# x turned by VectorE in 32x32 blocks that the store puts in place, with g moved into the division of x^T and a longer first phase

## The chip, the cores and the metric

One core of one Trainium2 chip. The metric is the time of one launch on the device in microseconds (us); the profile's span, without the launch's own ends, is about 1.8 us shorter. A ratio of two kernels is the mean time of one's fast runs over that of the other's fast runs of the same rounds, so it is not quite the ratio of the medians that stand beside it.

## The reference

```python
# q, k, v: (8, 8, 576, 64) float32; w_in (512, 2048), w_out (2048, 512): float64
kv  = einsum('bhsd,bhse->bhde', k, v)
o   = einsum('bhsd,bhde->bhse', q, kv)
o   = o / sqrt(mean(o * o, -1) + 1e-6) * g_norm             # g_norm: (64,)
x   = o.transpose(0, 2, 1, 3).reshape(4608, 512)
h   = x @ w_in
out = (maximum(h, 0) + log1p(exp(-abs(h)))) @ w_out         # softplus
```

## The kernel before

The 4608 rows are 36 tiles of 128, and 12 blocks of three tiles. The 2048 columns of the MLP are 16 chunks of 128. A *step* is one chunk of one block: 12 matmuls of 128x384 (L558; three factors of x^T and w_in for precision), softplus on ScalarE, a division of the result into three factors, and nine matmuls of 128x512 (L565). There are 192 steps, in three phases of 4, 6 and 6 chunks for all blocks; partial sums wait in DRAM between phases. Attention for all tiles is done in the first phase beside the steps, and x^T goes to DRAM, from which each later use loads it.

```python
PHASES = [range(0, 4), range(4, 10), range(10, 16)]
...
def split(ph, t, x, ready, pos):            # the division of x^T into three factors
    def high(): nc.scalar.activation(cols(0, F32R), x.tile, func=AF.Copy, scale=DOWN)                            # L410
    def low():  nc.vector.tensor_tensor(out=cols(1, F32R), in0=x.tile, in1=cols(0), op=ALU.subtract)             # L413
    def less(): nc.vector.scalar_tensor_tensor(out=cols(2, F32R), in0=cols(1), scalar=-RADIX, in1=cols(0), ...)  # L416
...
def rows(t):                                # attention of one tile
    def turn_q():                           # L490: four transposes on TensorE
    def out_rows():                         # L496: q^T by kv
    def norm():  nc.vector.tensor_tensor(out=x.tile, in0=o.tile, in1=r.tile..., op=ALU.mult)                     # L507
    def turn_x():
        y = new(xp, [P, KD, P])
        for p in range(KD):
            nc.tensor.transpose(y[:, p], pairs(x.tile, p), ident)                                                # L512
    ...
    a = add("PE", 440, turn_x, [a], pos + 0.5, [xp], [x])
    a = add("ACT", 700, lambda: nc.scalar.activation(new(xg, [P, KD, P]), xp.tile, func=AF.Identity, scale=g_col), ...)  # L526
    x_there[t] = add("SP", 350, lambda: nc.sync.dma_start(out=xd[t], in_=xg.tile.rearrange("p a t -> p (a t)")), ...)
    if t < AT_ONCE:                         # the first six tiles are divided at once, without DRAM
        split(0, t, xg, a, pos + 0.5)
def x_again(ph, t):                         # load x^T from DRAM and divide it
    ld = add("SP", 350, lambda: nc.sync.dma_start(out=new(xt, ...), in_=xd[t]), ...)
    split(ph, t, xt, ld, pos)
```

Every operation is recorded with a *position* (in steps). A small list scheduler in the kernel then orders each engine's instructions by buffers and positions at build time. The list `P0` holds the fitted positions: when each weight is fetched and converted, how early x is made. Tiles that TensorE writes lie in PSUM (the pool `ps` in the kernel), the others in SBUF (`sb`). Filler matmuls (L668) occupy TensorE where it has nothing else to do before the first step.

## Time and profile before

| | before |
|---|---|
| median of the first session, us | 938.43 |
| TensorE busy in the span of 936.5 us | 925.1 |
| TensorE idle from the first step (45.6 us) to the end of the first phase | 0.2 |
| DMA engines busy | 47% |
| first phase ends | 336 us |

### The profile page before, as it was taken

What the parts mean: (1) busy time and instruction counts of PE and PEld (TensorE: products, weight loads), DVE (VectorE), ACT (ScalarE), POOL (GpSimd) and SP (SyncE); (2) the same over time, 40 slices, a digit from 0 to 9 for tenths busy, and PEclk for the clock granted to TensorE, in tenths of its full rate; (3) what the DMA queues carried; (4) which work ended last, traced back from release to release, by engine and by line L of the source; (5) the groups of instructions that cost most, each with busy time, mean ns of one, the idle gap of its engine ahead of it and who ended that gap; (6) DMA issues with size and microseconds to landing.
All of it is one profiled execution on the core that took longest, in us unless ns stands there. A gap on an engine that the chain in (4) does not pass through costs nothing.

```text
span 936.5 us, 13571 instructions
## 1 busy us (share of the span) xinstructions
PE 925.1 (99%) x5019; PEld 837.3 (89%) x5019; DVE 601.5 (64%) x1045; ACT 449.3 (48%) x871; POOL 66.9 (7%) x42
## 2 busy tenths in 40 slices
PE   7999999999999999999999999999999999999998
PEld 5799999999999899989999999899999999999997
DVE  7888876777777667776767645485455554545443
ACT  5877766666666555544444332374323233232331
POOL 0331122212222000000000000000000000000000
PEclk9999999999999999999999999999999999999999
DMA  9999776786564444444343322343323333222221
GB/s 247 242 258 278 201 215 202 216 229 186 169 189 137 135 147 124 147 135 148 125 138 130 129 81 85 135 147 101 102 101 101 102 101 102 101 84 95 77 82 68
DMA packets 148673, 135.63 MB, mean 145 GB/s; under 512 B 86400, under 2 KB 102784, under 8 KB 148608
## 3 DMA queue, kind: packets, MB, share of 16 engines
q1 hardware_dynamic: 148448, 134.78, 47.0%
q8 instruction: 39, 0.64, 0.3%
q14 instruction: 26, 0.21, 0.1%
q10 hardware_dynamic: 160, 0.00, 0.0%
HBM read 93.85 MB, written 40.89 MB: 144 GB/s over the span
## 4 chain that ended last, share of the span: by engine, by line
PE 95%; DMA 2%; DVE 1%; ACT 1%; issue 0%; SPq 0%; ACTq 0%
PE h L558 43%; PE s L565 42%; PE o L472 3%; PE o L496 3%; PE tp L512 2%; PE tp L490 1%; DMA kvt<-in_v_dram 1%; DMA raw<-in_moe_w_out_dram 1%; DMA part<-xg 0%; PE s L496 0%; PE h L668 0%; DVE xv L413 0%; PE h L357 0%; DVE xv L416 0%; SPq L456 0%
## 5 line engine op out<-in xcount | busy, mean ns | idle before, releaser
L565 PE MATMUL s<-w,gv 128*128 128x512 f32 x1728 | 438.8, 396 | 0.0
L558 PE MATMUL h<-xv,w 128*128 128x384 f32 x2304 | 435.8, 337 | 0.0
L558 PEld LDWEIGHTS h<-xv,w 128*128 128x128 f32 x2304 | 405.6, 188 | 14.1
L565 PEld LDWEIGHTS s<-w,gv 128*128 128x128 f32 x1728 | 318.1, 188 | 57.1 <-issue 0.3
L578 ACT ACTIVATE g<-h 128x384 f32<-128x384 f32 x192 | 94.5, 492 | 393.4 <-PE h L558 380.7
L569 DVE TENSOR_TENSOR gv<-g,gv 128x384 fp32r<-128x384 f32 x192 | 107.0, 557 | 203.2 <-ACT gv L580 202.5
L573 DVE SCALAR_TENSOR_TENSOR gv<-gv 128x384 fp32r<-128x384 f32 x192 | 107.1, 558 | 6.2
L580 ACT ACTIVATE gv<-g 128x384 fp32r<-128x384 f32 x192 | 101.0, 526 | 6.7 <-PE s L565 1.2
L504 POOL TENSOR_TENSOR r<-r,half 128x8 f32<-128x8 f32 x36 | 66.2, 1840 | 228.8 <-DVE r L501 223.3
L413 DVE TENSOR_TENSOR xv<-xt,xv 128x512 fp32r<-128x512 f32 x102 | 70.1, 687 | 17.8 <-ACT xv L410 17.5
L416 DVE SCALAR_TENSOR_TENSOR xv<-xv 128x512 fp32r<-128x512 f32 x108 | 74.6, 691 | 3.2
L410 ACT ACTIVATE xv<-xt 128x512 fp32r<-128x512 f32 x102 | 62.6, 623 | 16.0 <-DMA xt<-x 16.0
L605 DVE SCALAR_TENSOR_TENSOR qT<-s,kvt 128x512 f32<-128x512 f32 x36 | 24.7, 687 | 28.2 <-PE s L565 26.0
L472 PE MATMUL o<-kvt,kvt 128*128 128x128 f32 x256 | 35.0, 281 | 3.7 <-DMA kvt<-in_v_dram 3.7
L472 PEld LDWEIGHTS o<-kvt,kvt 128*128 128x128 f32 x256 | 33.4, 195 | 5.8 <-issue 3.2
L496 PE MATMUL o<-kv_diag,qT 128*128 128x128 f32 (+1 forms) x296 | 36.9, 276 | 0.3 <-DVE kv_diag L480 0.3
L496 PEld LDWEIGHTS o<-kv_diag,qT 128*128 128x128 f32 (+1 forms) x296 | 34.4, 179 | 1.4 <-issue 0.6
L500 DVE TENSOR_REDUCE r<-x 128x8 f32<-128x512 f32 x36 | 24.6, 684 | 9.0 <-ACT x L520 8.7
L526 ACT ACTIVATE xg<-tp,g_col 128x512 f32<-128x512 f32 x36 | 24.7, 687 | 10.1 <-PE tp L512 9.8
L507 DVE TENSOR_TENSOR x<-o,r 128x512 f32<-128x512 f32 x33 | 22.7, 689 | 8.5 <-POOL r L504 8.2
L605 DVE SCALAR_TENSOR_TENSOR qT<-s,scale,kvt 128x512 f32<-128x512 f32 x12 | 9.0, 752 | 29.4 <-PE s L565 29.4
L515 ACT COPY qT<-tp 128x512 f32<-128x512 f32 x36 | 21.1, 586 | 11.2 <-PE tp L490 10.9
(68 smaller groups left out, 508.4 us busy)
## 6 DMA issues: line engine op xcount, KB each, us to landing
xt<-x SPq DMA_DIRECT2D x102, 256.0 KB, 2.9
kvt<-part SPq DMA_DIRECT2D x72, 256.0 KB, 4.2
x<-xg SPq DMA_DIRECT2D x36, 256.0 KB, 3.2
part<-xg SPq DMA_DIRECT2D x36, 256.0 KB, 3.3
part<-qT SPq DMA_DIRECT2D x36, 256.0 KB, 2.0
raw<-in_moe_w_in_dram SPq DMA_DIRECT2D x16, 512.0 KB, 5.3
kvt<-in_k_dram SPq DMA_DIRECT2D x64, 128.0 KB, 4.1
kvt<-in_v_dram SPq DMA_DIRECT2D x32, 256.0 KB, 4.1
```

The lines of the kernel that those rows point to most:

```text
L410: nc.scalar.activation(cols(0, F32R), x.tile, func=AF.Copy, scale=DOWN)
L413: nc.vector.tensor_tensor(out=cols(1, F32R), in0=x.tile, in1=cols(0), op=ALU.subtract)
L416: nc.vector.scalar_tensor_tensor(out=cols(2, F32R), in0=cols(1), scalar=-RADIX, in1=cols(0), op0=ALU.mult, op1=ALU.add)
L472: nc.tensor.matmul(kv[:, i if tail else p], lhsT=l, rhs=r, start=(p == 0 and i == 0), stop=tail, skip_group_check=True)
L496: nc.tensor.matmul(pairs(y[r0:r0 + n], p), lhsT=qT.tile[:, p, r0:r0 + n], rhs=kv_diag[b % 2][:, p], start=(p == 0), stop=True, skip_group_ ...
L504: nc.gpsimd.tensor_tensor(out=r.tile, in0=r.tile, in1=half, op=ALU.pow)
L558: nc.tensor.matmul(hp, lhsT=w_in.tile[:, i, kd * P:(kd + 1) * P], rhs=xv.tile[:, i, kd], start=(m == 0), stop=(m == 3 * KD - 1))
L565: nc.tensor.matmul(mine[i].tile, lhsT=gv.tile[:, m, i * P:(i + 1) * P], rhs=w_out.tile[:, m], start=(c == cs[0] and m == 0), stop=(c == cs ...
L569: nc.vector.tensor_tensor(out=gv.tile[:, 1], in0=g.tile, in1=gv.tile.bitcast(F32)[:, 0], op=ALU.subtract)
L573: nc.vector.scalar_tensor_tensor(out=gv.tile[:, 2], in0=f32[:, 1], scalar=-RADIX, in1=f32[:, 0], op0=ALU.mult, op1=ALU.add)
L578: a = add("ACT", 490, lambda: nc.scalar.activation(new(g, [P, NT]), h.tile, func=AF.Softplus, scale=1.0 + E), [a], s, [g], [h])
L580: a = add("ACT", 530, lambda: nc.scalar.activation(new(gv, [P, 3, NT], F32R)[:, 0], g.tile, func=AF.Copy, scale=DOWN), [a], s, [gv])
```

## The change

Intent: take x's transposes off TensorE, the bound, and spread attention, which loads VectorE and the DMA engines, over more steps.

```diff
-    PHASES = [range(0, 4), range(4, 10), range(10, 16)]
+    LATE = 4
+    ENDS = [[0] * n_blocks, [4] * LATE + [6] * (n_blocks - LATE), [10] * n_blocks, [KF] * n_blocks]
+    CHUNKS = {(ph, n): range(ENDS[ph][n], ENDS[ph + 1][n]) for ph in PHASES for n in range(n_blocks)}
-    P0 = [31 positions]
+    P0 = [40 positions, most of the first 16 changed]
@@ split
-            nc.scalar.activation(cols(0, F32R), x.tile, func=AF.Copy, scale=DOWN)
+            nc.scalar.activation(cols(0, F32R), x.tile, func=AF.Identity, scale=g_down)
-            nc.vector.tensor_tensor(out=cols(1, F32R), in0=x.tile, in1=cols(0), op=ALU.subtract)
+            nc.vector.scalar_tensor_tensor(out=cols(1, F32R), in0=x.tile, scalar=g_col, in1=cols(0),
+                                           op0=ALU.mult, op1=ALU.subtract)
@@ rows
         if t < AT_ONCE:
-            split(0, t, xg, a, pos + 0.5)
+            a = add("PE", 440, turn_x, ...)                     # as before for tiles 0 to 5
+            split(0, t, xp, a, pos + 0.5)
+            a = add("ACT", 600, lambda: nc.scalar.copy(new(xg, [P, KD, P]), xp.tile), ...)
+            x_there[t] = [add("SP", 450, lambda: nc.sync.dma_start(
+                out=xd[t].rearrange("(a p) t -> p a t", p=P), in_=xg.tile), ...)]
+            return
+        def turn_blocks():
+            nc.vector.transpose(out=new(xg, [P, d_model]), in_=x.tile.rearrange("p h d -> p (h d)"))
+        def store(r0):
+            nc.sync.dma_start(out=xd[t][:, r0:r0 + BL].rearrange("(b i) j -> i b j", i=BL),
+                              in_=xg.tile[r0:r0 + BL].rearrange("i (b j) -> i b j", j=BL))
+        a = add("DVE", 690, turn_blocks, [a], pos, [xg], [x])
+        x_there[t] = [add("SP", 450, lambda r0=r0: store(r0), ...) for r0 in range(0, P, BL)]
```

In the changed kernel L578 and L585 are the matmuls of a step, L519 and L544 the two ways of turning x, L416, L419 and L423 the division, L535 the copy for tiles 0 to 5, L547 the blockwise store, L556 the reload.

More of the change, by code (lines that the diff above doesn't have):

```diff
@@ L22 @@
 DOWN = 1.0 - 2.0 ** -13
+DOWN_G = 1.0 - 0.99 * 2.0 ** -13
 E = 1.0 / RADIX
@@ L174 @@
     n_blocks = n_tokens // NT
+    LATE = 4
     n_tiles = n_tokens // P
-    PHASES = [range(0, 4), range(4, 10), range(10, 16)]
+    ENDS = [[0] * n_blocks, [4] * LATE + [6] * (n_blocks - LATE), [10] * n_blocks, [KF] * n_blocks]
+    PHASES = range(len(ENDS) - 1)
+    CHUNKS = {(ph, n): range(ENDS[ph][n], ENDS[ph + 1][n]) for ph in PHASES for n in range(n_blocks)}
     PLACES = 8
-    LAST = len(PHASES) - 1
-    P0 = [-57.5, -0.2, -24.8, -1.2, -4.6, 5.5, -63.4, 1.2, -34.0, -33.3, -32.7, -11.2, -17.2, -25.2, 23.8, -3.7,
-          1.0, -9.5, 6.5, 7.0, 7.0, 24.5, -0.5, 2.5, 2.5, 8.5, -9.5, 5, 9, 67.5, 8]
-    CONVERT, FETCH, EARLY = P0[:8], P0[8:16], P0[16:]
+    LAST = PHASES[-1]
+    P0 = [-53.0, -6.2, -18.3, -1.2, -9.1, 4.0, -38.9, 0.2, -43.0, -32.8, -31.7, -14.2, -15.7, -21.2,
+          2.8, -3.7, 1.0, -9.5, 7.0, 7.0, 7.0, 24.5, -0.5, 2.5, 2.0, 16.5, -13.0, 4.5, 16.5, 21.5, 27.0,
+          42.5, 44.0, 66.5, 72, 80, 88, 96.5, 102.0, 3]
+    CONVERT, FETCH, EARLY, LATER = P0[:8], P0[8:16], P0[16:27], P0[27:]
     AT_ONCE = 2 * TB
@@ L194 @@
     g_col = const.tile([P, 1], F32, name="g_col")
+    g_down = const.tile([P, 1], F32, name="g_down")
     half = const.tile([P, H], F32, name="half")
@@ L218, in pairs @@
         return x[:, 2 * p:2 * p + 2].rearrange("r h d -> r (h d)")
-    ORDER = [(ph, n, c) for ph, cs in enumerate(PHASES) for n in range(n_blocks) for c in cs]
-    phase_of = {c: ph for ph, cs in enumerate(PHASES) for c in cs}
+    ORDER = [(ph, n, c) for (ph, n), cs in CHUNKS.items() for c in cs]
     first_step = {}
@@ L312, in weight @@
             d3 = add("DVE", 690, mask, [d2, a1], pos, [])
-            over_done.append(add("ACT", 910, beyond, [d3], pos + (4 if c in PHASES[0] else 0), [], [sq]))
+            over_done.append(add("ACT", 910, beyond, [d3], pos + (4 if c < 4 else 0), [], [sq]))
             d4 = add("DVE", 430, power, [d3], pos, [p, w])
@@ L319, in weight @@
                         [f], pos, [w], [raw])
-        if c < PLACES or phase_of[c] - phase_of[c - PLACES] > 1:
+        if c < PLACES or first_step[c] - last_step[c - PLACES] > 30:
             divide(j, w, ready, pos, "p", c < 4)
@@ L385 @@
     first_tile = [b * S // P for b in range(B)]
-    xd = [dram.tile([P, KD * P], F32, name=f"x{t}") for t in range(n_tiles)]
+    xd = [dram.tile([d_model, P], F32, name=f"x{t}") for t in range(n_tiles)]
     x_there = {}
@@ L419, in split @@
         before = x_split.get((ph, n), [None])[-1:]
-        a = add("ACT", 640, high, [ready] + ([] if i == 0 else [first_high[ph, n]]), pos, [dst] if i == 0 else [])
+        a = add("ACT", 700, high, [ready] + ([] if i == 0 else [first_high[ph, n]]), pos, [dst] if i == 0 else [])
         if i == 0:
             first_high[ph, n] = a
-        b = add("DVE", 700, low, [a], pos, [], [x])
+        b = add("DVE", 740, low, [a], pos, [], [x])
         c = add("DVE", 700, less, [b], pos)
@@ L524, in rows @@
         a = add("DVE", 700, norm, [a, o_task], pos, [], [o, r])
-        a = add("PE", 440, turn_x, [a], pos + 0.5, [xp], [x])
-        a = add("ACT", 700, lambda: nc.scalar.activation(new(xg, [P, KD, P]), xp.tile, func=AF.Identity, scale=g_col),
-                [a], pos + 0.5, [xg], [xp])
-        x_there[t] = add("SP", 350, lambda: nc.sync.dma_start(out=xd[t], in_=xg.tile.rearrange("p a t -> p (a t)")),
-                         [a], pos + 0.5, [], [xg], 900)
-        if t < AT_ONCE:
-            split(0, t, xg, a, pos + 0.5)
+        if t < AT_ONCE:
+            a = add("PE", 440, turn_x, [a], pos + 0.5, [xp], [x])
+            split(0, t, xp, a, pos + 0.5)
+            a = add("ACT", 600, lambda: nc.scalar.copy(new(xg, [P, KD, P]), xp.tile), [a], pos + 1, [xg], [xp])
+            x_there[t] = [add("SP", 450, lambda: nc.sync.dma_start(
+                out=xd[t].rearrange("(a p) t -> p a t", p=P), in_=xg.tile), [a], pos + 1, [], [xg], 950)]
+            return
+        BL = 32
+        def turn_blocks():
[4 more added lines that the diff above has]
+        a = add("DVE", 690, turn_blocks, [a], pos, [xg], [x])
+        x_there[t] = [add("SP", 450, lambda r0=r0: store(r0), [a], pos + 0.5, [], [xg], 450) for r0 in range(0, P, BL)]
     def x_again(ph, t):
@@ L535, in x_again @@
         xt = slot("xt")
-        ld = add("SP", 350, lambda: nc.sync.dma_start(out=new(xt, [P, KD, P]).rearrange("p a t -> p (a t)"), in_=xd[t]),
-                 [x_there[t]], pos - EARLY[9], [xt], [], 900, behind=first_step[ph, t // TB] - 5)
+        ld = add("SP", 350, lambda: nc.sync.dma_start(out=new(xt, [P, KD, P]), in_=xd[t].rearrange("(a p) t -> p a t", p=P)),
+                 x_there[t], pos - EARLY[9], [xt], [], 900, behind=first_step[ph, t // TB] - 5)
         split(ph, t, xt, ld, pos)
@@ L546, in step @@
         ph, n, c = ORDER[s]
-        cs = PHASES[ph]
+        cs = CHUNKS[ph, n]
         h, g, gv = slot("h"), slot("g"), slot("gv")
@@ L627 @@
         nc.scalar.dma_start(out=g_col[e * D:(e + 1) * D], in_=g_norm.rearrange("(d one) -> d one", one=1))
+    nc.scalar.mul(g_down, g_col, DOWN_G)
     nc.scalar.preload_act_table_set("softplus")
@@ L636 @@
         nc.vector.memset(x, 0.0)
-    EACH = (first_step[PHASES[1][0]] - EARLY[12]) / len(PHASES[1])
     for c in range(KF):
         for j in (2 * c, 2 * c + 1):
-            if c in PHASES[0]:
-                pos = CONVERT[j]
-            elif c in PHASES[1]:
-                pos = EARLY[11] + EACH * (c - PHASES[1][0] + 0.5 * (j % 2))
-            else:
-                pos = first_step[PHASES[2][0]] - EARLY[13] + EARLY[14] * (c - PHASES[2][0]) + EARLY[14] / 2 * (j % 2)
-            weight(j, pos, FETCH[j] if c in PHASES[0] else pos)
+            pos = CONVERT[j] if c < 4 else LATER[c - 4] + LATER[12] * (j % 2)
+            weight(j, pos, FETCH[j] if c < 4 else pos)
     for b in range(B):
@@ L652 @@
                 rows(t)
-    for ph in range(len(PHASES)):
+    for ph in PHASES:
         for n in range(n_blocks):
@@ L658 @@
     for s in range(len(ORDER)):
-        if s == first_step[PHASES[2][0]]:
+        if s == first_step[LAST, 0]:
             whole_scale(s - 4)
```

## The prediction

938.4 - 12.8 - 1 + 1.5 comes to 926.1, put down as 926 us. The 0.69 us for a block turn, from which it reckons VectorE's load, was the author's estimate. In the trace of before, three of VectorE's operations of 128x512, L413, L507 and L416, took 687, 689 and 691 ns.

> **What bounds the kernel now.** I read the page's engine table and the strips over 40 slices first, then the table of stretches, the chain of work that ended last, TensorE's part of the timeline, the waits, the groups by shape, and the DMA view of two windows.
>
> ```profile
> span 936.5 us, 13571 instructions
> PE 925.1 (99%) x5019; PEld 837.3 (89%) x5019; DVE 601.5 (64%) x1045; ACT 449.3 (48%) x871; POOL 66.9 (7%) x42
> ...
> DVE  7888876777777667776767645485455554545443
> ...
> DMA  9999776786564444444343322343323333222221
> ```
>
> TensorE is busy for 99% of the span, while VectorE (DVE) and the DMA engines are high only in the left third, the stage in which attention makes x. Busy is not yet bound, so the stretches (us, then each engine's busy time, the clock, the DMA share and GB/s):
>
> ```profile
> 0.00:45.60 45.60, 38.09 (x227) 29.38 (x228) 36.08 (x68) 31.71 (x59) 7.85 (x10) 1.00 0.98 245
> 45.60:120.00 74.40, 74.40 (x487) 69.32 (x486) 62.10 (x113) 54.71 (x108) 18.64 (x10) 1.00 0.90 240
> 120.00:200.00 80.00, 79.82 (x511) 73.47 (x511) 58.98 (x106) 51.65 (x101) 16.70 (x9) 1.00 0.74 210
> 200.00:336.00 136.00, 136.00 (x802) 124.79 (x801) 93.41 (x167) 85.45 (x166) 23.72 (x13) 1.00 0.54 168
> 336.00:936.50 600.50, 596.78 (x3000) 540.37 (x2998) 350.96 (x593) 225.74 (x440) 0.00 (x0) 1.00 0.33 111
> ```
>
> At 45.6 us the first MLP step begins, at 336 us the last eviction of the first phase. From the first step on TensorE never pauses (its idle time in the waits view is about 0.2 us), at the full granted clock. So after 45.6 us every TensorE instruction taken out comes off the end, and nothing taken from another engine does, unless TensorE is made to wait. Before 45.6 us the DMA engines are full (0.98) and TensorE runs filler (L668).
>
> The chain within 45.6 to 336 us says what TensorE does there:
>
> ```profile
> by line: PE h L558 34.6%; PE s L565 33.7%; PE o L496 9.7%; PE o L472 8.6%; PE tp L512 4.9%; PE tp L490 4.2%; DMA part<-xg 1.4%; ACT xg L599 0.4%; issue 0.3%; PE h L356 0.2%; PE h L357 0.2%; DVE p L341 0.2%; DVE x L507 0.2%; DVE xv L413 0.2%
> ```
>
> L512, the turning of x, is 4.9% of 290.4 us, 14.2 us, for the 32 tiles turned there: 0.44 us a tile. The timeline confirms it (start, length, ...):
>
> ```profile
> 81.46 0.60 PE L512 MATMUL tp<-ident_r,x 128*128 128x128 f32 x4
> 81.90 1.06 PE L496 MATMUL o<-kv_diag,qT 128*128 128x128 f32 x8
> ...
> 92.90 0.60 PE L512 MATMUL tp<-ident_r,x 128*128 128x128 f32 x4
> 93.25 0.48 PE L565 MATMUL s<-w,gv 128*128 128x512 f32 x1
> ```
>
> The four transposes of a tile are shown as 0.60 us, but the next work starts 0.44 or 0.35 us after them, since matmuls overlap. That slot, about 0.41 to 0.44 us, is what a tile is worth, not 0.60 and not four times the 273 ns of one.
>
> [...] the trace has 273 ns, but the slots show about 0.1 us each in a row. [...] the trace's L507 of that shape took 689 ns. [...] I estimate 0.69 us for the 128x512 block transpose; no run has it yet. [...] The trace has short packets only as loads, so it cannot tell what 128 B writes cost.
>
> **The change part by part.**
>
> *Turning.* Tiles 6 to 35 lose their L512: 30 tiles x 0.41 to 0.44 us = 12.3 to 13.2 us of TensorE, all after the first step, all on the path. Tiles 0 to 5 keep it. ScalarE (ACT) loses 30 of
>
> ```profile
> L526 ACT ACTIVATE xg<-tp,g_col 128x512 f32<-128x512 f32 x36 | 24.7, 687 | 10.1 <-PE tp L512 9.8 <-DMA q<-in_q_dram 0.3
> L410 ACT ACTIVATE xv<-xt 128x512 fp32r<-128x512 f32 x102 | 62.6, 623 | 16.0 <-DMA xt<-x 16.0
> L413 DVE TENSOR_TENSOR xv<-xt,xv 128x512 fp32r<-128x512 f32 x102 | 70.1, 687 | 17.8 <-ACT xv L410 17.5
> ```
>
> that is 20.6 us, and VectorE gains 30 x 0.69 = 20.7 us. Both lie beside TensorE.
>
> *g in the division.* L410 gets a per-partition scale in place of a constant; L526, which has one, took 687 against 623 ns, so 108 x 0.064 = 7 us more on ScalarE, off the path. L413 becomes a scalar_tensor_tensor, and L416 of that kind takes 691 against 687 ns: nothing.
>
> *Stores and loads of x.* A tile's store goes from 128 packets of 2 KB to four DMAs with 2048 packets of 128 B; each reload from 128 of 2 KB to 512 of 512 B. Two windows give the price of a packet:
>
> ```profile
> DMA packets 43122, 20.08 MB, mean 251 GB/s; under 512 B 34702, under 2 KB 41325, under 8 KB 43115
> q1 hardware_dynamic: 42955, 19.99, 98.9%
> ...
> q1 hardware_dynamic: 5184, 9.44, 28.4%
> ```
>
> (the first two rows are 0 to 80 us, the last is 700 to 800 us). Engine time is share x window x 16: 1266 us and 454 us. Fitted as a per packet plus b per byte, 42955a + 19.99Mb = 1266 and 5184a + 9.44Mb = 454 give a = 9.5 ns and b = 0.043 ns/B: 15 ns for 128 B, 31.5 for 512 B, 97 for 2 KB. A blockwise store then costs 2048 x 15 / 16 = 1.9 us of all 16 engines against 0.8 us; 30 of them add 34 us. Reloads cost 1.0 against 0.8 us: 102 x 0.23 = 23 us. Fewer weights are spilled (the built program has 8 spills for 12, each a store and a load), about -6 us. Together some +52 us on the present 440 (47% of 936), so 53% over the whole run.
>
> *Six chunks from the fifth block on.* The number of steps stays 192, with the same matmuls, so TensorE's sum does not move. The first phase has 4x4 + 8x6 = 64 steps in place of 48, which at about 4.17 us a step (100 us hold 504 matmuls of 21 per step late in the run) is 67 us longer, less the 13 us: it ends near 390. VectorE's load up to there is today 36.1+62.1+59.0+93.4 = 250.6 of 336 us, 75%; after, 250.6 + 20.7 + 16 x 1.115 (L569 and L573 of one step) = 289 of 390, 74%. DMA today is 44.7+67.0+59.2+73.4 = 244 us, 73%; after, 244 + 34 + about 8 for the reloads there = 286, again 73%. The longer phase thus pays for what the first part loads onto the two.
>
> *Start.* By the built program's order the first step comes after the third x tile is turned, not the fourth, and after three fewer units of attention output; about 4 us of TensorE work is moved past it, so an earlier start is mostly given back. The split of the first tiles reads the PSUM result without L526 before it, which shortens that latency by 0.7 us per tile. ScalarE gets a second table load (1.28 us) at a time when it waits for data. I put the start's net gain at 0 to 2 us.
>
> Sum: 938.4 - 12.8 - 1 (start) + 1.5 (new small waits) = 926 us.
>
> **Rivals.** (1) *128 B writes are much dearer than the line says.* If each took 30 ns, a store would be 3.8 us and a DMA share of 0.90 to 0.98, as in the first 120 us, would go over 1 while blocks 2 to 4 are made (there the program places 28 us of DMA work by my packet prices within four steps, which last about 24 us). x would come late and TensorE wait: 10 to 20 us lost, 930 to 945. For it: [...] the full DMA strip early. Against: loads of 256 B fit the line, and 30 stores spread over 64 steps. (2) *VectorE becomes the bound early.* A tile costs it 3.6 us (L500 0.68, L501 0.17, L507, the turn, L413 and L416 0.69 each), so in blocks 0 to 3 it has 3 x 3.6 us a block for x and 4 x 1.1 for the steps, about 15 in the block's 24 us, and four or five weight matrices in those 96 us at 5 us each (eight instructions of 0.42 or 0.69 us): 90%. Before, 62.1 of 74.4 us (83%) gave no TensorE wait. Queueing behind weights could cost 2 to 6 us: 928 to 932. (3) *The start gains more than I give it*, since filler and DMA fill the first 45 us and the order of weights was set anew: 918 to 922. (4) *The turn was hidden anyway*: refuted by the absence of TensorE idle time; then the time would stay at 938.
>
> **Range and chances.** The 12.8 us is read straight from TensorE's slots, so it is nearly sure; what may spoil it are rivals 1 and 2, what may add is rival 3. 2% is 18.8 us, more than the transposes are worth, so faster by over 2% (below 919.7) needs 6 us from the start: 0.11. Slower by over 2% needs 30 us of new waits: 0.02. Range 918.5 to 934.
>
> **What would show it.** Right: the x transpose group has 24 instead of 144 instructions; TensorE's busy time is near 913; its waits after the first step stay under 3 us; the block transpose takes about 690 ns; the DMA share up to 120 us stays at or below 0.98 and packets total some 247,000; steps outside the first phase keep 4.17 us. Wrong: TensorE idle on VectorE's x or on an x load between 50 and 150 us, a block store landing much later than 5 us, or a first step more than 3 us away from 45.6.

## The result and the profile after

The changed kernel took 927.27 us (median of 4, 926.81 to 927.35) against 938.88 us; the ratio is 0.9876, 95% interval 0.9859 to 0.9893. That is 1.2% faster, within the 2% that counts as the same.

The page's engine table and two of its strips, kernel after:

```profile
span 925.6 us, 13404 instructions
PE 912.6 (99%) x4897; PEld 825.6 (89%) x4897; DVE 625.0 (68%) x1075; ACT 441.8 (48%) x843; POOL 63.9 (7%) x42
...
DVE  6888858886567864788688887584555555454553
...
DMA  9998798767667534233554565522333333332221
```

TensorE's busy time fell by 12.5 us (925.1 to 912.6), the span by 10.9. VectorE's rose by 23.5 us and its busy part reaches further right, as the longer first phase would have it.

From the first step to the end of the first phase (columns as in the prediction), before and then after:

```profile
45.60:336.00 290.40, 290.22 (x1797) 267.58 (x1796) 214.49 (x385) 191.81 (x373) 59.06 (x32) 1.00 0.69 198
```

```profile
42.20:390.00 347.80, 346.46 (x2035) 317.60 (x2035) 258.41 (x458) 198.07 (x383) 56.88 (x33) 1.00 0.68 168
```

TensorE's idle time there went from 0.2 to 1.3 us. VectorE's share is 74% in both, the DMA share 69% and 68%: the longer phase did pay for the added load. What TensorE waited for, by the waits view from 42 us on (engine, what, for whom: us, times, longest), is small and mixed:

```profile
PEld s L585 <- ACT xg L619: 0.9, 1, 0.9
PEld tp L497 <- PE h L363: 0.9, 1, 0.9
PE s L585 <- ACT xg L619: 0.7, 1, 0.7
```

The first step begins earlier (TensorE's timeline, before and then after; each window cuts the group of 12):

```profile
45.61 1.64 PE L558 MATMUL h<-xv,w 128*128 128x384 f32 x8
```

```profile
42.22 1.98 PE L578 MATMUL h<-xv,w 128*128 128x384 f32 x10
```

That is 3.4 us, yet from the first step to the end the kernel gained only 7.5 us (890.9 to 883.4), not the 12.8 us of the transposes: the built order moves three units of attention output (about 0.9 us each), one turn of q, one of x and one pair of weight matmuls past the first step, 4.1 us together by an estimate from these slots, and waits add 1.2 us (-12.8 + 4.1 + 1.2 = -7.5). The early start is work put off, not work saved.

The groups that changed, kernel after (busy us, mean ns | idle before):

```profile
L419 DVE SCALAR_TENSOR_TENSOR xv<-xt,g_col,xv 128x512 fp32r<-128x512 f32 x102 | 76.2, 747 | 19.9 <-ACT xv L416 19.6
L416 ACT ACTIVATE xv<-xt,g_down 128x512 fp32r<-128x512 f32 x102 | 72.5, 714 | 29.1 <-DMA xt<-x 29.0
...
L544 DVE STREAM_TRANSPOSE xg<-x 128x512 f32<-128x512 f32 x30 | 21.2, 708 | 6.2 <-DMA x<-xg 5.3 <-DMA part<-xg 0.6
...
L519 PE MATMUL tp<-ident_r,x 128*128 128x128 f32 x24 | 3.7, 277 | 0.2 <-DVE x L514 0.2
```

x's transposes on TensorE are 24 instructions in place of 144. The DMA queue (packets, MB, share of 16 engines), before and then after:

```profile
q1 hardware_dynamic: 148448, 134.78, 47.0%
```

```profile
DMA packets 248033, 133.53 MB, mean 144 GB/s; under 512 B 149152, under 2 KB 220832, under 8 KB 247968
...
q1 hardware_dynamic: 247808, 132.68, 51.8%
```

99,000 packets more for fewer bytes; the queue's engine time rose from 440 to 479 us, 39 us.

### The profile page after: what moved, and what is told of

It is laid out like the page before. It is cut to its first block, busy times and chain, and to the rows that moved or that the text cites. A ratio compares the mean times of both kernels' runs of the same rounds, so it can differ in the third digit from the quotient of the medians.

```text
span 925.6 us, 13404 instructions
## 1 busy us (share of the span) xinstructions
PE 912.6 (99%) x4897; PEld 825.6 (89%) x4897; DVE 625.0 (68%) x1075; ACT 441.8 (48%) x843; POOL 63.9 (7%) x42
## 3 DMA queue, kind: packets, MB, share of 16 engines
q1 hardware_dynamic: 247808, 132.68, 51.8%
## 4 chain that ended last, share of the span: by engine, by line
PE 92%; DMA 4%; SPq 2%; DVE 1%; issue 0%; ACT 0%; DVEq 0%; ACTq 0%
PE h L578 42%; PE s L585 41%; PE o L479 3%; PE o L503 3%; PE tp L497 2%; DMA kvt<-in_v_dram 1%; DMA part<-xg 1%; SPq L547 1%; DMA x<-xg 1%; DMA q<-in_q_dram 1%; PE h L683 0%; SPq L463 0%; DVE xg L544 0%; DMA xt<-x 0%; PE s L503 0%
## 5 line engine op out<-in xcount | busy, mean ns | idle before, releaser
L578 PE MATMUL h<-xv,w 128*128 128x384 f32 x2304 | 436.0, 337 | 0.0
L585 PE MATMUL s<-w,gv 128*128 128x512 f32 x1728 | 432.9, 394 | 0.7 <-ACT xg L619 0.7
L578 PEld LDWEIGHTS h<-xv,w 128*128 128x128 f32 x2304 | 405.2, 188 | 14.1 <-issue 0.7
L585 PEld LDWEIGHTS s<-w,gv 128*128 128x128 f32 x1728 | 320.1, 188 | 59.3 <-ACT xg L619 0.9
L419 DVE SCALAR_TENSOR_TENSOR xv<-xt,g_col,xv 128x512 fp32r<-128x512 f32 x102 | 76.2, 747 | 19.9 <-ACT xv L416 19.6
L416 ACT ACTIVATE xv<-xt,g_down 128x512 fp32r<-128x512 f32 x102 | 72.5, 714 | 29.1 <-DMA xt<-x 29.0
L511 POOL TENSOR_TENSOR r<-r,half 128x8 f32<-128x8 f32 x36 | 63.2, 1756 | 278.5 <-DVE r L508 278.5
L423 DVE SCALAR_TENSOR_TENSOR xv<-xv 128x512 fp32r<-128x512 f32 x108 | 74.5, 689 | 3.0
L503 PE MATMUL o<-kv_diag,qT 128*128 128x128 f32 (+1 forms) x296 | 36.9, 276 | 0.0
L507 DVE TENSOR_REDUCE r<-x 128x8 f32<-128x512 f32 x36 | 24.4, 677 | 17.0 <-ACT x L527 16.9
L503 PEld LDWEIGHTS o<-kv_diag,qT 128*128 128x128 f32 (+1 forms) x296 | 34.5, 179 | 1.5 <-issue 0.7
L527 ACT ACTIVATE x<-o 128x512 f32<-128x512 f32 x33 | 19.7, 597 | 16.1 <-PE o L503 14.1
L295 DVE SCALAR_TENSOR_TENSOR t<-sq,t 128x512 f32<-128x512 bf16 x32 | 22.1, 690 | 5.3 <-ACT sq L279 3.7
```

The lines of the kernel that those rows point to most:

```text
L416: nc.scalar.activation(cols(0, F32R), x.tile, func=AF.Identity, scale=g_down)
L419: nc.vector.scalar_tensor_tensor(out=cols(1, F32R), in0=x.tile, scalar=g_col, in1=cols(0), op0=ALU.mult, op1=ALU.subtract)
L503: nc.tensor.matmul(pairs(y[r0:r0 + n], p), lhsT=qT.tile[:, p, r0:r0 + n], rhs=kv_diag[b % 2][:, p], start=(p == 0), stop=True, skip_group_ ...
L511: nc.gpsimd.tensor_tensor(out=r.tile, in0=r.tile, in1=half, op=ALU.pow)
L578: nc.tensor.matmul(hp, lhsT=w_in.tile[:, i, kd * P:(kd + 1) * P], rhs=xv.tile[:, i, kd], start=(m == 0), stop=(m == 3 * KD - 1))
L585: nc.tensor.matmul(mine[i].tile, lhsT=gv.tile[:, m, i * P:(i + 1) * P], rhs=w_out.tile[:, m], start=(c == cs[0] and m == 0), stop=(c == cs ...
```

## The experiments

My theory: the gain is TensorE's removed slots and nothing else; the rest lies beside TensorE, as long as no new wait appears. Rivals: part of the gain comes from the longer first phase or the start; short packets or VectorE give part of it back. In the table the base is the kernel before on the same chip in the same rounds.

| run | median us | base us | ratio (95%) |
|---|---|---|---|
| change | 927.27 | 938.88 | 0.9876 (0.9859 to 0.9893) |
| e1 turned by TensorE | 939.11 | 939.04 | 0.9997 (0.9983 to 1.0012) |
| e2 four chunks for all | 931.00 | 939.04 | 0.9913 (0.9896 to 0.9929) |
| e3 phases and positions only | 939.84 | 939.47 | 0.9999 (0.9984 to 1.0014) |
| e4 old positions | 944.32 | 939.47 | 1.0050 (1.0037 to 1.0064) |
| e5 long packets | 926.28 | 939.04 | 0.9860 (0.9845 to 0.9875) |
| e6 turned twice | 928.64 | 939.04 | 0.9889 (0.9874 to 0.9903) |
| e7 weights' rest on VectorE | 931.19 | 939.47 | 0.9910 (0.9896 to 0.9923) |
| e9 only three tiles at once | 937.10 | 939.47 | 0.9972 (0.9959 to 0.9985) |
| e10 old weight positions | 944.38 | 938.55 | 1.0053 (1.0033 to 1.0072) |
| e11 old x positions | 925.56 | 938.55 | 0.9857 (0.9842 to 0.9871) |
| e12 q from tile 24 | 969.76 | 938.55 | 1.0325 (1.0309 to 1.0341) |
| e13 q from tile 30 | 947.44 | 938.55 | 1.0089 (1.0071 to 1.0106) |

### Undoing the turn, or keeping all but the turn (e1, e3)

```diff
-        if t < AT_ONCE:
+        if True:                                        # e1: every tile by TensorE, as tiles 0 to 5
             a = add("PE", 440, turn_x, [a], pos + 0.5, [xp], [x])
-            split(0, t, xp, a, pos + 0.5)
+            if t < AT_ONCE:
+                split(0, t, xp, a, pos + 0.5)
```

> The changed kernel with all 36 tiles turned by TensorE again (copied by ScalarE, stored in 512 B packets); g in the division, six chunks and the new positions stay. Theory (the gain is TensorE's slots alone): 30 x 0.41 to 0.44 us come back, TensorE busy 912.6 -> about 925, time 939 to 941, no better than before. Rival (part of the gain is the earlier start or the longer first phase): 930 to 937.

e3 is the kernel before (TensorE turns x, L526 multiplies by g, 2 KB packets) with the new `CHUNKS`, `P0` and rule for spills.

> The kernel before (x turned by TensorE, g in the copy from PSUM, 2 KB packets) with the new phases (six chunks from the fifth block) and the new positions. Theory (phases and positions move work but add or remove none on TensorE): 937.5 to 940, the same as before. Rival (the phases or the earlier first step carry part of the gain): 930 to 936.

Measured: 939.11 and 939.84 us, both level with the kernel before. TensorE's busy time, e1 and then e3:

```profile
PE 925.5 (99%) x5017; PEld 837.4 (89%) x5017; DVE 607.5 (65%) x1045; ACT 456.9 (49%) x873; POOL 66.0 (7%) x42
```

```profile
PE 925.7 (99%) x5018; PEld 836.7 (89%) x5018; DVE 601.5 (64%) x1045; ACT 450.1 (48%) x871; POOL 66.3 (7%) x42
```

Both read as the 925.1 us of before. With the turn undone, 11.8 us come back (927.27 to 939.11), all of the gain; with only the new phases and positions, there is no gain. The theory holds. The rival of a gain from phases or start falls with e1, which keeps both: its first step, at 41.7 us, is even earlier than the change's. e3 alone could not settle the start, since its first step is no earlier than the 45.6 us of before (e1, then e3):

```profile
41.72 2.32 PE L579 MATMUL h<-xv,w 128*128 128x384 f32 x12
```

```profile
46.66 2.33 PE L564 MATMUL h<-xv,w 128*128 128x384 f32 x12
```

e1 keeps g in the division, e3 does not, and they differ by 0.7 us with overlapping intervals: moving g, and with it the packets of 512 B, is neutral for the time.

### Room for the turn: the six chunks, VectorE, the packets (e2, e6, e5)

```diff
-    ENDS = [[0] * n_blocks, [4] * LATE + [6] * (n_blocks - LATE), ...]
+    ENDS = [[0] * n_blocks, [4] * n_blocks, ...]               # e2
```

> The changed kernel with four chunks in the first phase for every block; VectorE still turns x. Theory (six chunks only makes room for VectorE and DMA): TensorE busy stays at 912.6; the first phase is 16 steps shorter, so VectorE's share in it rises from 74% to some 86% and TensorE waits appear: 928 to 934. Rival A (it changes nothing, the gain is all the turn): 926.5 to 928. Rival B (it is what makes the turn worth anything): 935 or more.

Measured: 931.0 us, 3.7 us slower than the change. TensorE's busy time is 912.5 us, unchanged; what differs is waits. From 100 to 150 us, e2 and then the change:

```profile
100.00:150.00 50.00, 48.14 (x300) 43.93 (x299) 34.60 (x64) 25.19 (x47) 12.45 (x7) 1.00 0.83 194
```

```profile
100.00:150.00 50.00, 49.27 (x302) 45.08 (x301) 37.15 (x67) 26.79 (x53) 10.06 (x6) 1.00 0.84 201
```

TensorE is idle for 1.9 us there in e2 against 0.7 us, and for 0.9 us against none from 150 to 310 us; the longest kinds of wait in e2 are on loads of v (1.6 us on the load of weights into TensorE, the same pause seen again as 1.6 us on its matmul). So six chunks are worth about 4 us here. That this is room and nothing else is not shown: e2 keeps the positions that were fitted for six chunks, and its trace has 12 spills (converted weights put into DRAM and loaded again later) where the change has 8.

```diff
-            nc.vector.transpose(out=new(xg, [P, d_model]), in_=...)
+            new(xg, [P, d_model])
+            for _ in range(2):                                 # e6
+                nc.vector.transpose(out=xg.tile, in_=...)
```

> The changed kernel with every block turn of VectorE done twice, 30 x 0.7 = 21 us more VectorE work in the first phase, nothing else. Theory (VectorE works beside TensorE, share of the first phase 74% -> 80%): 927 to 931. Rival (VectorE is close to being the bound there): 937 or more, half of the 21 us or more on the end.

Measured: 928.64 us, 1.4 us slower, with VectorE busy 644.2 us instead of 625.0. Of 19 us of added work 1.4 reach the end by the medians, and the intervals of the two ratios overlap: VectorE has room for this.

```diff
-            nc.sync.dma_start(out=xd[t][:, r0:r0 + BL].rearrange("(b i) j -> i b j", i=BL),
-                              in_=xg.tile[r0:r0 + BL].rearrange("i (b j) -> i b j", j=BL))
+            nc.sync.dma_start(out=xd[t].rearrange("(p a) t -> p (a t)", p=P)[r0:r0 + BL],   # e5
+                              in_=xg.tile[r0:r0 + BL])
```

(and the reload likewise; the blocks are then not placed, so the result is wrong: its relative error is 0.78.)

> The changed kernel, same order of instructions, but x goes to DRAM and back in contiguous 2 KB packets (result wrong on purpose: blocks are not placed). Theory (DMA has room): packets fall from 248,000 to about 148,000, DMA time of q1 from 51.8% to about 47%, time 925.5 to 927.5. Rival (short packets give back part of the gain): 920 to 924.

Measured: 926.28 us, 1.0 us less by the medians, with ratios whose intervals overlap. The queue:

```profile
q1 hardware_dynamic: 151040, 132.68, 47.9%
```

96,768 packets fewer for the same bytes, and 36.6 us less of all 16 engines (51.8% of 925.6 less 47.9% of 924.6). The DMA engines have that room; about 1 us of it reaches the end, by the medians. The same sum prices the two kinds of packet. The queues of e1 and then e3:

```profile
q1 hardware_dynamic: 200288, 132.68, 47.9%
```

```profile
q1 hardware_dynamic: 147296, 132.68, 46.0%
```

e1 stores its tiles in 512 B packets and has 47,520 packets fewer than the change and 30.6 us less: 10 ns of one engine for each packet more when 512 B are cut into 128 B (and a tile is stored by four DMAs in place of one). e1 against e3 is the same set of DMAs with x moved in 512 B instead of 2 KB: 52,992 packets more and 16.9 us, 5 ns for each. e1 against e5 gives only 6 us for 49,248 packets, but e5 stores a tile in four DMAs of 32 rows where e3 uses one of 128, so e3 is the cleaner base. Why e5 lies 11 us above e3 is not explained.

### The positions (e4, e10, e11)

```diff
-    P0 = [-53.0, -6.2, -18.3, ...                             # 40 positions
+    P0 = [-57.5, -0.2, -24.8, ...                             # e4: the first 27 as before
```

> The changed kernel with the first 27 of its positions set back to those of before (when weights of the first four chunks are fetched and converted, how early x is made). Theory (the positions are a fitting that takes small waits away, the start gives back what it gains): 927.5 to 931. Rival (the new start is worth several us): 932 or more.

Measured: 944.32 us, a miss: 17 us slower than the change and 5 slower than the kernel before. The whole gain, and more, hangs on the fitted positions. A line of the waits view of e4:

```profile
PE h L360 <- ACT w L342: 4.9, 1, 4.9
```

(TensorE waiting for a weight's conversion.) e10 sets back the 16 positions of the first eight weights, of which 14 differ, e11 the 11 that say how early x and its inputs are made, of which four differ.

> The old positions cost 17 us (944.3 against 927.3), where 0 to 4 were expected; the trace of that run shows TensorE waiting 4.9 us at 93 us for the first step of one weight's conversion and 7 us between 68 and 80 us for VectorE's normalisation of x. This run sets back only the 16 positions of the first eight weights. Theory (a weight of chunk 3 is fetched too late behind the four stores per tile, so its conversion falls where VectorE is fullest): nearly all of it, 940 to 945, with the 4.9 us wait there. Rival (it is when x is made): 927 to 930.

> The other half: only the 11 positions that say how early x and its inputs are made are set back. Theory: 927 to 930. Rival: 940 to 945.

Measured: e10 944.38 us, e11 925.56 us. The weights' positions, taken together, are the whole of it. Two stretches of 20 us, e10 and then the change:

```profile
60.00:80.00 20.00, 15.41 (x97) 13.97 (x95) 16.57 (x30) 10.60 (x22) 5.73 (x4) 0.83 0.95 231
80.00:100.00 20.00, 14.85 (x67) 13.29 (x68) 15.49 (x28) 9.38 (x18) 5.52 (x3) 0.74 0.41 85
```

```profile
60.00:80.00 20.00, 19.56 (x141) 18.92 (x140) 16.62 (x31) 13.78 (x29) 3.75 (x2) 1.00 0.99 234
80.00:100.00 20.00, 20.00 (x119) 17.66 (x118) 18.61 (x34) 12.72 (x25) 5.43 (x4) 1.00 0.67 163
```

TensorE is idle for 9.7 us of these 40 in e10 and for 0.4 us in the change, and the granted clock (the number after the five engines) is 0.83 and 0.74 there. What TensorE does is slower too: from 60 to 100 us an attention matmul of L501 takes 328 ns on average in e10, and 274 ns in the change (L503). Its busy time over the whole run is 920.4 us with the same instructions but for two filler matmuls, 7.8 us more. Idle time came with nearly as much again in slower work in this run. When the clock falls is not settled: e4 has 5.9 us of idle time from 60 to 80 us at a clock of 1.00, and 5.5 us from 80 to 100 us at 0.74.

Why idle: the fourth fetch of w_in is issued at 65.6 us in e10 and at 50.3 us in the change, the fourth of w_out at 59.6 and 51.4 us. Their conversion, 5 us of VectorE each, then falls on 65 to 82 us, and the block turns begin at 69 us. The chain of work of e10 from 76 to 90 us runs through VectorE for most of its pieces: the sum of squares (L505), the normalisation (L512), the turn (L542) and the weights' words (L301, L306, L309) one after another, with 1.96 us of the root on GpSimd, before TensorE may go on. The cause I had written down for e10 is half right: the weights do come late, but the single wait of 4.9 us is not in that run; several of 0.5 to 2.4 us on x, the kv copy, the copy of q and the division of x (L417, which now reads the one PSUM buffer that the turns of q need) take its place. It also overstated e4: the waits view there has 4.2 us on x, not 7. That the two late fetches are what counts among the 14 positions is read from the trace, not tested alone. How the 17 us divide between VectorE, the DMA queue and the clock is not settled.

e11 is at least as good as the change, and its TensorE waits are shorter, but the intervals overlap. It lies below its own forecast of 927 to 930. I do not call it a better version.

### Attempts to gain more (e7, e9, e12, e13)

```diff
-            divide(j, w, ready, pos, "p", c < 4)
+            divide(j, w, ready, pos, "p", j in (0, 1, 2, 4))   # e7: after the first step, VectorE takes a weight's rest
```

> An attempt to gain more by the same reasoning: the changed kernel, with the rest of those four weight matrices whose rest TensorE takes after the first step (two matmuls of 128x512 each, 0.23 to 0.32 us) taken by VectorE instead. Theory (TensorE's slots are the time, VectorE has room): 4 x about 0.55 = 2.2 us less, 925 to 926. Rival (VectorE is 90% busy just there and makes TensorE wait): 927 to 929.

Measured: 931.19 us, worse than both forecasts. One wait of TensorE, for VectorE's normalised x, is there that the change has not:

```profile
PE o L480 <- DVE x L515: 3.6, 1, 3.6
```

```diff
-    AT_ONCE = 2 * TB
+    AT_ONCE = TB                                               # e9: tiles 3 to 5 go over DRAM too
```

> An attempt to gain more: the changed kernel, with tiles 3 to 5 also turned by VectorE and brought back from DRAM, so that only the first block is turned by TensorE. Theory: 3 x 0.44 = 1.3 us less on TensorE, 926. Rival (the way over DRAM is longer than the time to block 1's first step, some 23 us, on full DMA engines): TensorE waits, 928 to 935.

Measured: 937.10 us, worse than both forecasts. Most of the gain is lost between 60 and 80 us:

```profile
60.00:80.00 20.00, 12.65 (x65) 11.29 (x64) 16.72 (x31) 9.31 (x18) 4.99 (x3) 0.66 0.93 209
```

TensorE is idle for 7.4 us there, 6.7 of them on loads of v, q and the tail of v, and the clock is 0.66. What delays the loads is not shown: the DMA share, 0.93, is no higher than the change's 0.99, but in the timeline of the queue that issues the DMAs the stores of four tiles fill 12.8 us from 52.6 to 72.3 us.

e12 and e13 turn q by VectorE as well, for tiles 24 to 35 or 30 to 35, late enough to be clear of the full early part. The load places the blocks, with at least 16 DMAs for a tile in these two kernels; whether fewer would do was not shown.

```diff
+            src = q[b, z // 2::2, s0:s0 + n, 32 * (z % 2):32 * (z % 2) + 32].rearrange("p (b i) j -> i p b j", i=32)
+            for g in range(NP):                                # for each of the four quadrants z
+                nc.sync.dma_start(out=y[:, g, r0 // 32:r0 // 32 + n // 32], in_=src[:, g])
...
+            a = add("DVE", 710, lambda: nc.vector.transpose(out=new(qT, ...), in_=q_s.tile), [ld], ...)
```

> An attempt to gain more late in the first phase, where VectorE and DMA are less full: q of tiles 24 to 35 turned by VectorE too, its blocks placed by the load (16 loads of 128 B pieces a tile[...]). Theory: 12 x 0.41 to 0.44 = 5 us less on TensorE, 922 to 923. Rival (the queue that issues the DMAs becomes the bound: 16 x about 0.45 = 7 us a tile beside some 5 us of other issues, in about 10 us a tile): TensorE waits for q or x, 930 or more.

> The same for tiles 30 to 35 only. Theory: 6 x 0.42 = 2.5 us less, 924.5 to 925. Rival (issue bound): 927 or more.

Measured: 969.76 and 947.44 us, the worst of all. In e12 the DMA-issuing queue (SP) works without a break while TensorE waits (timeline of the queue, and a line of the waits view):

```profile
317.68 10.29 SPq L417 DMA_DIRECT2D q<-in_q_dram  x22
328.01 0.43 SPq L268 DMA_DIRECT2D raw<-in_moe_w_in_dram  x1
328.54 3.30 SPq L417 DMA_DIRECT2D q<-in_q_dram  x7
```

```profile
PE o L519 <- DVE qT L541: 27.1, 4, 10.5
```

22 issues in 10.3 us are 0.47 us each, 7.5 us for a tile's 16. VectorE itself waits 27.9 us for these loads, while the DMA engines are busy for 0.43 of the stretch from 300 to 350 us. The bound there has become a queue that no busy share on the page shows.

No version beat the change beyond its interval.

## Why the prediction was right

- **TensorE is the bound and a slot is worth 0.41 to 0.44 us.** Right: 12.8 us were put down; TensorE's busy time fell by 12.5 us, and e1, which undoes the turn (and with it the 128 B stores), gives back 11.8 us of time. Reading 0.60 us from the timeline's lengths would have given 18 us.
- **The turn on VectorE, g and the stores lie beside TensorE.** Right, by e6 and e5: about 1.4 and 1.0 us reach the end by the medians, neither clear of the intervals.
- **Small new waits, 1.5 us.** Measured 1.2 us more of TensorE idle after the first step in the first phase. That this held was partly luck: it holds for the positions that the kernel came with, whose fit the prediction did not examine. With the old ones (e10) TensorE is idle for 9.2 us more than in the change.
- **The start, a gain of 0 to 2 us, 1 in the sum.** The first step moved by 3.4 us, more than the 3 us that the prediction had named as a sign of being wrong; but the 4 us of work moved past it were foreseen, and the net is about nothing. e1, whose first step is at 41.7 us, shows no gain from it. This term, and a base that was 0.45 us higher in the second session, make up the difference between 926.0 and 927.3.
- **Durations.** The block turn took 708 ns for an estimated 690. L416 took 714 ns, not 687: the estimate borrowed a row that reads PSUM, and for tiles 0 to 5, where L416 reads PSUM too, it took 686. L410, in the kernel before, which reads SBUF with a constant as its scale and Copy for Identity, took 623, 91 ns less. L419 was put down as "nothing", and took 747 for 687 ns, while L423, of the same operation and size with an immediate, took 689; the page of before had such a form, L605 with a scale from SBUF, at 752 ns. About 6 us of VectorE work were missed, off the path.
- **Packets.** +52 us of DMA time were put down, 39 came: the reloads were over-sized (23 us put down; at the 5 ns of e1 against e3 they come to 12), the stores right (34 put down; 31 for the step from 512 to 128 B alone). The fit's 9.5 ns for a packet, from the trace of before, stands beside the 10 ns of e1 against the change. The total of 247,000 packets is 248,000. The DMA share up to 120 us was to stay at or below 0.98; it is 1.00 up to 42.2 us and 0.89 from 45.6 to 120 us.
- **First phase.** It was to end near 390 us with VectorE at 74% and DMA at 73%. By the last eviction of a first-phase block it ends at 392 us; VectorE had 290 us of busy time up to 390 for a predicted 289, and the DMA share up to there is 0.72.
- **Rivals.** Dear 128 B writes (1) fell with e5. VectorE as the early bound (2) did not happen, but e10 shows how close it is: with the weights' old positions the chain runs through VectorE from 76 to 90 us, in a run that is 17 us slower; how much of this is VectorE's is open. The prediction gave the rival 2 to 6 us. A larger start (3) and a turn that was hidden anyway (4) both fell with e1.

What the prediction did not see is that the fit of the positions is a condition of the gain. It took them as a matter of the start alone.

## What to carry to other kernels

When one engine is busy from end to end (TensorE for 925.1 of 936.5 us here), price a change by that engine's slots, the distance from one start to the next (0.41 to 0.44 us for a tile's transposes, not the 0.60 us of their length), and ask of everything else only whether it makes that engine wait. Average shares alone do not show that work moved to another engine is free: VectorE's was 74% in the first phase before and after, but e10's new idle time of TensorE lies in 60 to 100 us (9.7 us), where VectorE is busy for 35.2 of 40 us in the change, and there the order of unrelated work (here the positions of eight weights, with two fetches 8 and 15 us later) cost 17 us in e10, more than the 12 us that the change gains. And when blocks are placed by DMAs, count the issues: in e12 the queue that issues them took 0.47 us for each and worked without a break from 317.7 to 331.8 us while TensorE waited, and the run was 42.5 us slower than the change.
